# Thirty-two tile transposes taken off TensorE: VectorE turns 32 by 32 blocks, DMA through DRAM puts the blocks in place

## The chip, the cores and the metric

The kernel runs on one core of one Trainium2 chip. The metric is the device time of the launch in microseconds, median of the runs; lower is better. The profile is one execution of the program with the hardware profiler on.

## The reference, cut to what matters

Three blocks follow one another on four sequences of 576 tokens with 512 channels, all in 32-bit floats.

```python
# attention with a threshold: only scores within tau of the row's maximum count
attn_out = _attn_ref(q, k, v, tau)
...
# channel block
u = x + real(fft(fft(x, axis=1), axis=2))
un = (u - mean(u)) / sqrt(var(u) + 1e-06)          # over the 512 channels
x3 = u + relu(un @ w_ch1) @ w_ch2                  # 512 -> 2048 -> 512
# token block
theta = x3 @ w_theta
y = w_tok_r @ (x3 * cos(theta)) + w_tok_i @ (x3 * sin(theta))   # over the 576 tokens
u = x3 + y
out = u + relu(u @ w_ch)
```

## The kernel before, in words

**Arithmetic.** Matrix products are done in a rounded 32-bit form. Each operand is split into a high part (a rounding cast on ScalarE) and a low part (a subtraction on VectorE or GpSimd), and a product takes three passes: high by high, high by low, low by high.

**Stages.** Attention runs over 16 pairs of heads, with the Fourier transforms of the four sequences woven in (`attention_and_fft`). Its result u goes to DRAM as 18 tiles of 128 tokens by 512 channels (`u_d`, stores L876 and L921). `channel_mlp` reads them back in five chunks (`CHUNKS`, of 4, 4, 4, 3 and 3 tiles). `token_mix` reads the 18 tiles of its result x3 (`x3_d`) and works sequence by sequence, b = 0 to 3.

**A layer-norm tile** (`norm`, L1088 to L1144) is loaded into one of two buffers `un` (L1096), gets its statistics on VectorE (L1101, L1102), a root on GpSimd (L1106 to L1108) and its scaling on ScalarE or VectorE (L1113, L1115). Four TensorE transposes of 128 by 128 (L1120) put its channels on the partitions, in one PSUM bank; ScalarE casts the bank to the high part `uh` (L1127) and VectorE subtracts for the low part `ul` (L1131). `uh` and `ul` of a chunk lie in tiles b16 and b17, or b18 and b19, by turns.

**The channel products** (`unit`) go over 16 slices f of the hidden 2048 in each chunk. `first` is 12 matmuls (L1158) into a bank h. ScalarE makes `hh` of it (relu and cast, L1163), VectorE makes `hl` (L1167). `second` is three matmuls for each tile of the chunk (L1178 to L1180). On TensorE's queue, which runs in order, first(f+1) stands ahead of second(f). After slice 15, `leave` adds the reloaded u on VectorE (L1208) and stores the x3 tile (L1211).

**A token tile** (`token`, L1272 onward) is loaded from `x3_d` into `tok` (L1280), turned by four TensorE transposes (L1285), split into `xs` high and low (L1289 on ScalarE, L1292 on VectorE), and copied turned into `x3T` for the sequence (L1298, for the two tail tiles L1302). The theta product is 12 matmuls (L1310); then come five VectorE steps (L1314 to L1329), three ScalarE steps (L1332 to L1338), two products with the unturned tile (L1342) and the split into z (L1380, L1383). `mix` multiplies z by the token weights (L1434, 216 matmuls for each sequence), adds into `x3T` in place (L1452 to L1455) and splits the sum (L1468 to L1479). `final` is 12 matmuls at a time (L1498) whose result is added to `x3T` on VectorE (L1505 to L1510) and stored (L1513). `x3T` has two places, b18 and b16, so sequence 2 takes over the place of sequence 0, and 3 that of 1.

**Order.** Nothing is issued in source order. Each piece of work is an operation with the engines that may do it, a cost, a priority, what it comes after and which buffers it makes or uses (`Plan.op`, L130). `Plan.schedule` (L137) plays the program through with these costs and fixes for every engine, SyncE's DMA queue (SP) among them, one order; each queue then runs in that order and waits on semaphores. A tile load is entered as 800 ns of SP with a `delay` of 2500 ns until it has landed. `SHIFT` (from L1578 on) is a table of some 400 offsets that are added to priorities. `Plan.PORT` (L106) names the operations in which VectorE and GpSimd are not planned at the same time.

Of the kernel before, what the change touches and what calls it, by code (L numbers as in the profile page):

```python
# [9 lines left out]
F32 = mybir.dt.float32  # L10
# [88 lines left out]
class Plan:  # L99
# [888 lines left out]
def channel_mlp(pl, tc, ident, tb, pss, P2, wf, u_d, x3_d, w3, w3_d):  # L988

    nc = tc.nc  # L990
    for t, n in dict(raw2=2, rawe=1, ve=1, v0=1, v1=1, sh=1, un=2, hh=2, hl=2, hh2=2, hl2=2).items():
        pl.tag(t, n)
# [3 lines left out]
    wt, X, acc, R = {}, {}, {}, {}  # L996
# [88 lines left out]
    def stored(t):  # L1085
        return [("us", t)] if t < 16 else [("us", t, 0), ("us", t, 1)]

    def norm(ci, j, p0):  # L1088
# [47 lines left out]
        pl.op(("nl", k), "SP", 800, p0, load, stored(t), [u], delay=2500)  # L1136
        pl.op(("n0", k), "DVE", 830, p0 + 1, stats, [("nl", k)], (), [u])
        pl.op(("n1", k), "POOL", 1400, p0 + 1, root, [("n0", k)])
        pl.op(("n2", k), (("ACT", act(512, False)), ("DVE", 460)), 0, p0 + 2, scale, [("n1", k)], (), [u])
        pl.op(("n3", k), "PE", 428, p0 + 3, turn, [("n2", k)] + ([("first", (ci - 2, NF - 1))] if ci > 1 else []) +  # L1140
# [54 lines left out]
    def leave(ci):  # L1195
# [29 lines left out]
def token_mix(pl, tc, ident, tb, pss, P2, w3_d, x3_d, out):  # L1225
# [46 lines left out]
    def token(t, p0):  # L1272
# [3 lines left out]
        T, O = ("O", "T", "tok", t), ("O", "tok", t)  # L1276
# [5 lines left out]
        def turn(e):  # L1282
            loc["T"] = pl.bank([128, 4, 128], f"xT{t}")
            for c in range(4):
                e.transpose(loc["T"][:, c], loc["t"][:, 0, c * 128:c * 128 + 128], ident[:])  # L1285

        def hi(e):
            loc["x"] = new("v0", [128, 2, 4, 128], f"xs{t}", F32R)
            e.copy(loc["x"][:, 0], loc["T"][:])  # L1289

        def lo(e):
            e.tensor_sub(loc["x"][:, 1], loc["T"][:], f32(loc["x"][:, 0]))  # L1292

        def keep(e):
            if i < 4:
                if i == 0:
                    xT[b] = new(X_TAG[b % 2], [128, 4, 512], f"x3T{b}")
                e.copy(xT[b][:, :, i * 128:i * 128 + 128], loc["T"][:])  # L1298
            else:
                if t == 16:  # L1300
                    XT[0] = new("v1", [128, 4, 256], "xtail")
                e.copy(XT[0][:, :, 64 * b:64 * b + 128], loc["T"][:])  # L1302
# [114 lines left out]
    def mix(b, c, halves):  # L1417
# [31 lines left out]
        def add(e):  # L1449
# [3 lines left out]
            if 1 in halves:  # L1453
# [5 lines left out]
              [("mix", b, c, halves, 8), ("tk", 16 + b // 2)] + [("tk", 4 * b + i) for i in range(4)], (), [ps, xtile(b), XTT])  # L1459
# [78 lines left out]
class Late:  # L1538
# [186 lines left out]
    (('bound', 15, 8), -199.02), (('bound', 2, 8), -206.66), (('bound', 3, 0), -61.74), (('bound', 3, 3), -109.26),  # L1725
    (('bound', 6, 6), -61.18), (('bound', 9, 2), -85.32), (('bound', 9, 5), 220.4), (('bound', None, 3), 53.52),
# [241 lines left out]
```

## Time and profile before

| what | value |
|---|---|
| median of 3 runs | 976.63 us (973.43 to 978.11) |
| the profiled execution, its own time | 976.14 us |
| its span, first to last instruction | 974.4 us |
| TensorE matmuls busy | 952.7 us (98%) |
| VectorE, ScalarE, GpSimd busy | 604.1, 449.7, 298.6 us |
| mean granted clock | 0.998 |

A matmul's duration in the profile covers its whole way through the array, and the next one starts before it ends. So the sum of durations counts overlaps twice, while the chain of waits gives each instruction the time that it alone adds. A group's row has its line, engine, operation, output and inputs, shapes and count, then busy time and mean, then idle time before it and what ended that. The windows' rows have, for each stretch, each engine's busy time and count, the granted clock, the mean share of the 16 DMA engines and GB/s.

### The profile page before, as it was taken

The page shows a single profiled execution, that of the slowest core. Times are in us where ns is not written, and L with a number is a line of the kernel's source. Part 1 is how long each engine was busy: PE and PEld are TensorE (multiplying, and loading weights), DVE is VectorE, ACT ScalarE, POOL GpSimd, SP SyncE. Part 2 cuts the span into 40 slices and gives each one's busy share as a digit, 9 for nine tenths or more (in the row PEclk, how much of TensorE's full clock was granted, in tenths as well). Part 3 has the DMA queues.
Part 4 walks back from the last instruction along what each step waited for, and adds up shares of the span by engine and source line. Part 5 has one row for each costly group of instructions (what it writes and reads, how often), then busy time and mean ns, then how long its engine had stood idle before and what let it go on. Part 6 is the DMA issues. An engine that isn't in the chain of part 4 may idle for free.

```text
span 974.4 us, 15966 instructions
## 1 busy us (share of the span) xinstructions
PE 952.7 (98%) x5874; PEld 819.9 (84%) x5874; DVE 604.1 (62%) x1206; ACT 449.7 (46%) x851; POOL 298.6 (31%) x457
## 2 busy tenths in 40 slices
PE   8899999999899999999999999999999999999998
PEld 6676788777778788888888888899988999999998
DVE  6777888898898898665432451311255478676633
ACT  7677877777877545433221321111143245352410
POOL 3375755657563774543300110000001011000100
PEclk9999999999999999999999999999999999999999
DMA  6798548755681566435733440100336101111011
GB/s 186 200 224 209 141 111 222 203 149 145 181 209 61 169 202 225 136 121 198 251 126 106 149 166 17 55 1 1 141 128 223 63 23 47 46 41 53 11 50 50
DMA packets 52142, 122.74 MB, mean 126 GB/s; under 512 B 9440, under 2 KB 14240, under 8 KB 51680
## 3 DMA queue, kind: packets, MB, share of 16 engines
q1 hardware_dynamic: 51040, 118.08, 41.1%
q0 software_dynamic: 720, 2.76, 1.1%
q8 instruction: 47, 0.77, 0.3%
q10 hardware_dynamic: 304, 0.87, 0.3%
q14 instruction: 31, 0.25, 0.1%
HBM read 68.95 MB, written 23.66 MB: 95 GB/s over the span
## 4 chain that ended last, share of the span: by engine, by line
PE 81%; DMA 4%; DVE 3%; ACT 1%; issue 1%; POOL 1%; SPq 0%; DVEq 0%; ACTq 0%
PE h L1158 20%; PE y L1434 12%; PE acc L1180 7%; PE acc L1179 7%; PE acc L1178 7%; PE f L1498 5%; PE th L1310 5%; PE O L571 5%; PE T L501 3%; PE ps L469 2%; DMA u_d<-u 2%; PE ps L470 2%; PE ps L464 1%; DMA mu<-u_d 1%; PE Xo L775 1%; DVE P L494 1%
## 5 line engine op out<-in xcount | busy, mean ns | idle before, releaser
L1158 PE MATMUL h<-uh,w 128*128 128x512 f32 (+1 forms) x640 | 198.6, 371 | 0.0
L1167 DVE SCALAR_TENSOR_TENSOR hl<-h,hh 128x512 fp32r<-128x512 f32 (+1 forms) x80 | 50.8, 637 | 170.6 <-ACT hh L1163 166.0
L1163 ACT ACTIVATE hh<-h 128x512 fp32r<-128x512 f32 (+1 forms) x80 | 44.4, 555 | 240.6 <-PE h L1158 180.7
L1158 PEld LDWEIGHTS h<-uh,w 128*128 128x128 f32 x640 | 118.9, 188 | 16.7
L494 DVE SCALAR_TENSOR_TENSOR P<-ps,c,P 128x576 f32<-128x576 f32 x144 | 115.3, 814 | 14.7 <-ACT P L483 10.4
L478 DVE TENSOR_REDUCE c<-ps 128x1 f32<-128x576 f32 x144 | 106.2, 751 | 25.5 <-PE ps L470 16.4
L1158 PE MATMUL h<-ul,w 128*128 128x512 f32 (+1 forms) x320 | 118.1, 369 | 0.0
L483 ACT ACTIVATE P<-ps,c 128x576 f32<-128x576 f32 x144 | 106.3, 751 | 19.2 <-DVE c L478 15.7
L1178 PE MATMUL acc<-w,hh 128*128 128x512 f32 x288 | 113.7, 395 | 0.0
L1180 PE MATMUL acc<-w,hl 128*128 128x512 f32 x288 | 112.9, 392 | 0.0
L1179 PE MATMUL acc<-w,hh 128*128 128x512 f32 x288 | 112.6, 391 | 0.0
L1434 PE MATMUL y<-w,z 128*128 128x288 f32 x768 | 109.3, 296 | 0.0
L1434 PEld LDWEIGHTS y<-w,z 128*128 128x128 f32 x768 | 104.2, 188 | 0.7
L501 PE MATMUL T<-ident,P 128*128 128x128 f32 x576 | 84.2, 275 | 6.4 <-ACT pt L510 2.3
L510 ACT COPY pt<-T 128x512 f32<-128x512 f32 (+1 forms) x160 | 83.8, 555 | 10.7 <-PE T L501 9.8
L571 PE MATMUL O<-pt,vr 128*64 128x320 f32 (+1 forms) x640 | 85.8, 415 | 0.5 <-ACT R L624 0.5
L501 PEld LDWEIGHTS T<-ident,P 128*128 128x128 f32 x576 | 66.4, 140 | 14.1 <-ACT pt L510 6.5
L469 PE MATMUL ps<-H,L 128*128 128x288 f32 x240 | 75.4, 331 | 1.3 <-DVE P L494 0.5
L571 PEld LDWEIGHTS O<-pt,vr 128*64 128x64 f32 x640 | 43.5, 138 | 32.1 <-issue 4.3
L1342 POOL TENSOR_TENSOR tok<-tok 128x512 f32<-128x512 f32 x5 | 6.5, 1298 | 204.1 <-ACT tok L1338 175.7
L1158 PEld LDWEIGHTS h<-ul,w 128*128 128x128 f32 x320 | 60.1, 188 | 8.5
L470 PE MATMUL ps<-X,L 128*128 128x288 f32 x240 | 66.9, 295 | 0.0
(354 smaller groups left out, 1738.0 us busy)
## 6 DMA issues: line engine op xcount, KB each, us to landing
raw<-in_qk SPq DMA_DIRECT2D x14, 608.0 KB
vr<-in_vv SPq DMA_DIRECT2D x16, 384.0 KB
w<-w_d SPq DMA_DIRECT2D x6, 992.0 KB
H<-hs SPq DMA_DIRECT2D x30, 160.0 KB
X<-raw SPq DMA_DIRECT2D x30, 160.0 KB
X<-hs SPq DMA_DIRECT2D x30, 160.0 KB
H<-raw SPq DMA_DIRECT2D x30, 160.0 KB
mu<-u_d SPq DMA_DIRECT2D x18, 256.0 KB
```

The costliest lines, as they stand in the source:

```text
L469: e.matmul(ps[:, half, :HS], L[:, qo:qo + 128], H[:, ko:ko + HS], start=(j == 0), stop=False)
L470: e.matmul(ps[:, half, :HS], L[:, qo:qo + 128], X[:, ko:ko + HS], start=False, stop=(j == n - 1))
L478: e.tensor_reduce(loc["c4"][:, 0:1], loc["ps"][:, :, :HS], axis=AXES.XY, op=ALU.max, negate=True)
L483: e.activation(halves(), loc["ps"][:, :, :HS], AF.Exp, bias=loc["c4"][:, 0:1], scale=1.0)
L494: e.scalar_tensor_tensor(halves(), loc["ps"][:, :, :HS], loc["c4"][:, 1:2], halves(), op0=ALU.is_ge, op1=ALU.mult, accum_out=st["sums"][:, ...
L501: e.transpose(T[:, kt * 128:(kt + 1) * 128], P[:, kt * 128:(kt + 1) * 128], ident[:])
L571: e.matmul(O[64 * h:64 * h + 64, :n], w, x, start=(kt == 0), stop=(kt == 4))
L1158: e.matmul(loc["ps"][:, :n], a, x[:, c, :n], start=(k == 0), stop=(k == 11))
L1178: e.matmul(a, hh[:, q], wh, start=(f == 0), stop=False)
L1179: e.matmul(a, hh[:, q], wl, start=False, stop=False)
L1180: e.matmul(a, hl[:, q], wh, start=False, stop=(f == NF - 1))
L1434: e.matmul(loc["ps"][:, half, :HS], z[:, cs], w, start=(n == 0 and m == 0), stop=(n == 8 and m == 2))
```

## The change

14 of the 18 layer-norm tiles (chunks 1 to 4) and all 18 token tiles are no longer turned by TensorE. VectorE transposes each 32 by 32 block of a tile in its place (`flip`, into a single buffer `ut`). Four DMAs (`unfold`) write the blocks to a DRAM tile of 512 by 128, in runs of 32 floats, so that the tile lies there transposed. One DMA reads it back (`fetch`). For a layer-norm tile it lands in `ul`; ScalarE casts it to `uh` and VectorE or GpSimd subtracts in place. For a token tile the flip and the four DMAs are issued behind the addition of L1208 at the end of the chunk; the fetch lands in `x3T` directly, the split reads it there, and the copies of L1298 and L1302 go. The unturned load (L1280) stays, and is now awaited by the first VectorE step after theta. The subtraction for `xs` low may run on GpSimd. Some 300 lines of offsets in `SHIFT`, over all stages and attention's operations among them, are replaced by others.

```diff
+def unfold(e, d, src):
+    for i in range(4):
+        e.dma_start(d[:].rearrange("(b r) (i k)->i r b k", r=32, i=4)[i],
+                    src[32 * i:32 * i + 32].rearrange("r (b k)->r b k", k=32))
...
+        if ci:
+            def flip(e):
+                loc["b"] = new("ut", [128, 512], f"un{t}")
+                e.transpose(loc["b"][:], loc["u"][:])
+            def put(e):
+                unfold(e, un_d[t], loc["b"])
+            def fetch(e):
...
+                e.dma_start(f32(X[ci][1][:, :, q]), un_d[t][:].rearrange("(c p) k->p c k", c=4))
+            def hi2(e):
+                e.copy(X[ci][0][:, :, q], f32(X[ci][1][:, :, q]))
+            def lo2(e):
+                uh, ul = X[ci]
+                e.tensor_sub(ul[:, :, q], f32(ul[:, :, q]), f32(uh[:, :, q]))
+            ut = ("ut", ("n", t))
+            pl.op(("nf", k), "DVE", dve(512), p0 + 3, flip, [("n2", k), "attention done"], [ut], [u])
+            pl.op(("ns", k), "SP", 2480, p0 + 3, put, [("nf", k)], (), [ut], delay=2500)
+            pl.op(("nt", k), "SP", 800, p0 + 3, fetch, [("ns", k)] + ([("first", (ci - 2, NF - 1))] if ci > 1 else []) +
...
+            pl.op(("n4", k), "ACT", act(512, False), p0 + 3, hi2, [("nt", k)], (), cs)
+            pl.op(("n5", k), (("POOL", pool(512)), ("DVE", dve(512))), 0, p0 + 3, lo2, [("n4", k)], (), cs)
+            return
...
+            def flip(e, j=j, t=t):
+                B[t] = new("ut", [128, 512], f"xt{t}")
+                e.transpose(B[t][:], R[ci][:, j])
+            def put(e, t=t):
+                unfold(e, xt_d[t], B[t])
+            ut = ("ut", ("x", t))
+            pl.op(("xf", t), "DVE", dve(512), p0 + 0.2, flip, [("x3", t)], [ut], [raw])
+            pl.op(("xp", t), "SP", 2480, p0 + 0.3, put, [("xf", t)], (), [ut], delay=2500)
...
-        def turn(e):
-            loc["T"] = pl.bank([128, 4, 128], f"xT{t}")
-            for c in range(4):
-                e.transpose(loc["T"][:, c], loc["t"][:, 0, c * 128:c * 128 + 128], ident[:])
+        def fetch(e):
+            if i == 0:
+                xT[b] = new(X_TAG[b % 2], [128, 4, 512], f"x3T{b}")
...
+            e.dma_start(here(), xt_d[t][:].rearrange("(c p) k->p c k", c=4))
         def hi(e):
             loc["x"] = new("v0", [128, 2, 4, 128], f"xs{t}", F32R)
-            e.copy(loc["x"][:, 0], loc["T"][:])
+            e.copy(loc["x"][:, 0], here())
...
-        op("tt", "PE", 428, p0 + 2, turn, [("tl", t)], [T], [tk])
-        op("th", "ACT", act(512), p0 + 2.1, hi, [("tt", t)], [xp], [T])
-        op("to", "DVE", dve(512), p0 + 2.2, lo, [("th", t)], (), [T, xp])
-        op("tk", "ACT", act(512), p0 + 2.3, keep, [("tt", t)] + before, fresh, [T] + ([] if fresh else [kept]))
+        op("tx", "SP", 800, p0, fetch, [("xp", t)] + before, fresh, [] if fresh else [kept], delay=2500)
+        op("th", "ACT", act(512, False), p0 + 2.1, hi, [("tx", t)], [xp], [kept])
+        op("to", pool_or_dve(512), 0, p0 + 2.2, lo, [("th", t)], (), [kept, xp])
```

## Rows read from the trace of the kernel before

**Rows 1.** The page: span, and busy time of each engine.
```profile
span 974.4 us, 15966 instructions
PE 952.7 (98%) x5874; PEld 819.9 (84%) x5874; DVE 604.1 (62%) x1206; ACT 449.7 (46%) x851; POOL 298.6 (31%) x457
```

**Rows 2.** The windows: attention, channel products, changeover, token stage.
```profile
0.00:330.00 330.00, 312.72 (x2341) 250.47 (x2342) 271.57 (x643) 250.60 (x512) 193.24 (x371) 0.99 0.67 173
330.00:700.00 370.00, 369.03 (x1760) 312.75 (x1759) 172.29 (x235) 102.53 (x149) 88.45 (x74) 1.00 0.38 129
700.00:765.00 65.00, 65.00 (x328) 57.48 (x327) 31.93 (x53) 23.71 (x42) 5.16 (x4) 1.00 0.42 147
765.00:965.00 200.00, 200.00 (x1408) 193.47 (x1408) 126.08 (x270) 72.83 (x148) 11.70 (x9) 1.00 0.13 38
```

**Rows 3.** The chain of waits, pieces in order of time (start, us, what).
```profile
443.85 0.44 PE uT L1120 x4
...
891.45 0.44 PE xT L1285 x4
```

**Rows 4.** Groups of TensorE: the token tiles' transposes, as durations.
```profile
L1285 PE MATMUL xT<-ident,tok 128*128 128x128 f32 x72 | 10.8, 272 | 0.0
```

**Rows 5.** The timeline of TensorE around one set of transposes (start, us).
```profile
613.06 0.60 PE L1120 MATMUL uT<-ident,mu 128*128 128x128 f32 x4
613.42 0.48 PE L1178 MATMUL acc<-w,hh 128*128 128x512 f32 x1
```

**Rows 6.** Groups of VectorE, ScalarE and GpSimd with tiles of 128 by 512.
```profile
L1383 DVE TENSOR_TENSOR z<-tok,z 128x512 fp32r<-128x512 f32 x24 | 18.1, 762 | 0.9 <-ACT z L1380 0.2
L1329 DVE TENSOR_SCALAR tok<-tok 128x512 f32<-128x512 f32 x18 | 7.6, 425 | 0.4
L1383 POOL TENSOR_TENSOR z<-tok,z 128x512 fp32r<-128x512 f32 x8 | 10.4, 1303 | 64.5 <-ACT z L1380 56.8 <-issue 7.7
L1289 ACT CAST xs<-xT 128x512 fp32r<-128x512 f32 x18 | 10.5, 586 | 30.6 <-PE xT L1285 20.1 <-PE th L1310 10.4
```

**Rows 7.** Groups behind `first` in a chunk of four tiles.
```profile
L1163 ACT ACTIVATE hh<-h 128x512 fp32r<-128x512 f32 x48 | 28.7, 599 | 147.7 <-PE h L1158 112.5 <-PE acc L1179 35.2
L1167 DVE SCALAR_TENSOR_TENSOR hl<-h,hh 128x512 fp32r<-128x512 f32 x48 | 33.0, 690 | 92.4 <-ACT hh L1163 87.8 <-PE uT L1120 4.4
```

**Rows 8.** The chain's `first` of two moments, and DMA share of the stretches around them.
```profile
489.24 2.72 PE h L1158 x12
...
597.33 2.76 PE h L1158 x12
...
488.00:502.00 14.00, 14.00 (x64) 11.58 (x62) 5.59 (x8) 4.34 (x5) 1.86 (x1) 1.00 0.45 145
596.00:604.00 8.00, 8.00 (x36) 6.52 (x35) 1.38 (x2) 1.20 (x2) 0.00 (x0) 1.00 0.00 0
```

**Rows 9.** Timelines of SyncE and VectorE: a load, and what awaits it.
```profile
580.80 0.32 SPq L1096 DMA_DIRECT2D mu<-u_d  x1
...
583.82 0.69 DVE L1101 BATCH_NORM_STATS2 bs<-mu 128x6 f32<-128x512 f32 x1 [1.53 <-DMA mu<-u_d]
```

**Rows 10.** What SyncE's queue waited for (us in total, times, longest).
```profile
SPq L1211 <- DVE ru L1208: 103.6, 18, 66.0
```

**Rows 11.** The page: the packets of SyncE's queue over the whole span.
```profile
q1 hardware_dynamic: 51040, 118.08, 41.1%
```

**Rows 12.** The DMA view of 38.9 to 39.3 us: 256-byte packets, 0.4 us of 16 engines.
```profile
DMA packets 82, 0.02 MB, mean 49 GB/s; under 512 B 81, under 2 KB 81, under 8 KB 82
q1 hardware_dynamic: 82, 0.02, 28.2%
```

**Rows 13.** Timelines of TensorE and ScalarE: theta of tile 8; its copy into x3T.
```profile
818.69 2.92 PE L1310 MATMUL th<-w,xs 128*128 128x512 f32 x12
...
831.22 0.59 ACT L1298 COPY x3T<-xT 128x512 f32<-128x512 f32 x1 [3.07 <-DVE o L1509]
```

More of the change, by code (lines that the diff above doesn't have):

```diff
@@ L985, with channel_mlp @@
          ("y", 1, 0): 20, ("y", 1, 1): 21, ("u", 1, 0): 22, ("u", 1, 1): 23}
-def channel_mlp(pl, tc, ident, tb, pss, P2, wf, u_d, x3_d, w3, w3_d):
+def unfold(e, d, src):
+    for i in range(4):
+        e.dma_start(d[:].rearrange("(b r) (i k)->i r b k", r=32, i=4)[i],
+                    src[32 * i:32 * i + 32].rearrange("r (b k)->r b k", k=32))
+def channel_mlp(pl, tc, ident, tb, pss, P2, wf, u_d, x3_d, w3, w3_d, un_d, xt_d):
     nc = tc.nc
-    for t, n in dict(raw2=2, rawe=1, ve=1, v0=1, v1=1, sh=1, un=2, hh=2, hl=2, hh2=2, hl2=2).items():
+    for t, n in dict(raw2=2, rawe=1, ve=1, v0=1, v1=1, sh=1, un=2, hh=2, hl=2, hh2=2, hl2=2, ut=1).items():
         pl.tag(t, n)
@@ L1135, in norm @@
         cs = [(a, ("c", ci)), (b, ("c", ci))]
-        pl.op(("nl", k), "SP", 800, p0, load, stored(t), [u], delay=2500)
-        pl.op(("n0", k), "DVE", 830, p0 + 1, stats, [("nl", k)], (), [u])
+        nl = ("Nl" if ci else "nl", k)
+        pl.op(nl, "SP", 800, p0, load, stored(t), [u], delay=2500)
+        pl.op(("n0", k), "DVE", 830, p0 + 1, stats, [nl], (), [u])
         pl.op(("n1", k), "POOL", 1400, p0 + 1, root, [("n0", k)])
         pl.op(("n2", k), (("ACT", act(512, False)), ("DVE", 460)), 0, p0 + 2, scale, [("n1", k)], (), [u])
+        if ci:
[5 more added lines that the diff above has]
+            def fetch(e):
+                if j == 0:
+                    X[ci] = (new(a, [128, 4, 512], f"uh{ci}", F32R), new(b, [128, 4, 512], f"ul{ci}", F32R))
+                e.dma_start(f32(X[ci][1][:, :, q]), un_d[t][:].rearrange("(c p) k->p c k", c=4))
[8 more added lines that the diff above has]
+            pl.op(("nt", k), "SP", 800, p0 + 3, fetch, [("ns", k)] + ([("first", (ci - 2, NF - 1))] if ci > 1 else []) +
+                  (["fft done"] if ci % 2 and not j else []) + ([("nt", (ci, 0))] if j else []), [] if j else cs, cs if j else [],
+                  delay=2500)
+            pl.op(("n4", k), "ACT", act(512, False), p0 + 3, hi2, [("nt", k)], (), cs)
+            pl.op(("n5", k), (("POOL", pool(512)), ("DVE", dve(512))), 0, p0 + 3, lo2, [("n4", k)], (), cs)
+            return
         pl.op(("n3", k), "PE", 428, p0 + 3, turn, [("n2", k)] + ([("first", (ci - 2, NF - 1))] if ci > 1 else []) +
@@ L1222, in channel_mlp, with token_mix @@
         leave(ci)
-def token_mix(pl, tc, ident, tb, pss, P2, w3_d, x3_d, out):
+def token_mix(pl, tc, ident, tb, pss, P2, w3_d, x3_d, xt_d, out):
     pl.tag("ul3", 1)
@@ L1280, in load, with here @@
             e.dma_start(loc["t"][:, 0], x3_d[t])
-        def turn(e):
-            loc["T"] = pl.bank([128, 4, 128], f"xT{t}")
-            for c in range(4):
-                e.transpose(loc["T"][:, c], loc["t"][:, 0, c * 128:c * 128 + 128], ident[:])
+        def here():
+            return xT[b][:, :, i * 128:i * 128 + 128] if i < 4 else XT[0][:, :, 64 * b:64 * b + 128]
+        def fetch(e):
+            if i == 0:
+                xT[b] = new(X_TAG[b % 2], [128, 4, 512], f"x3T{b}")
+            if t == 16:
+                XT[0] = new("v1", [128, 4, 256], "xtail")
+            e.dma_start(here(), xt_d[t][:].rearrange("(c p) k->p c k", c=4))
         def hi(e):
             loc["x"] = new("v0", [128, 2, 4, 128], f"xs{t}", F32R)
-            e.copy(loc["x"][:, 0], loc["T"][:])
+            e.copy(loc["x"][:, 0], here())
         def lo(e):
[L1292 to L1302, printed above, removed]
+            e.tensor_sub(loc["x"][:, 1], here(), f32(loc["x"][:, 0]))
         def theta(e):
@@ L1458, in mix @@
         pl.op(("y", b, c, halves), "DVE", sum((dve(HS), dve(n2) + dve(64))[half] for half in halves), p1, add,
-              [("mix", b, c, halves, 8), ("tk", 16 + b // 2)] + [("tk", 4 * b + i) for i in range(4)], (), [ps, xtile(b), XTT])
+              [("mix", b, c, halves, 8), ("tx", 16 + b // 2)] + [("tx", 4 * b + i) for i in range(4)] +
+              [("to", 16 + b // 2)] + [("to", 4 * b + i) for i in range(4)], (), [ps, xtile(b), XTT])
         for half in halves:
@@ L1733 @@
-    (('exp', 2), -15.61), (('exp', 2, 6), 12.94), (('exp', None, 1), 5.82), (('exp', None, 3), -36.91),
[10 rows of a table removed]
-    (('fh', 2, 'o', 0), -133.99), (('first', 0, 3), -830.59), (('first', 1), 34.88), (('first', 1, 0), -33.34),
-    (('first', 3), -12.53), (('first', 3, 0), -29.48), (('first', 4, 7), 28.8), (('first', None, 13), 7.61),
[3 rows of a table removed]
-    (('guard',), 5.4), (('guard', 10), 80.15), (('guard', 14), 38.44), (('guard', 3), -95.63), (('hh', 0), -25.85),
[13 rows of a table removed]
-    (('mix',), 4.26), (('mix', 0), -58.41), (('mix', 1, 0, (0, 1), 1), 36.65), (('mix', 1, 0, (0, 1), 7), 29.14),
@@ L1764 @@
-    (('mix', 1, 1, (0, 1)), 18.65), (('mix', 1, 1, (0, 1), 0), -48.46), (('mix', 1, 1, (0, 1), 5), -4.22),
-    (('mix', 1, 2, (0, 1), 7), 85.31), (('mix', 1, 3, (0, 1)), 27.13), (('mix', 1, 3, (0, 1), 8), 37.56),
-    (('mix', 1, None, (0, 1)), -0.94), (('mix', 2, 0), 16.76), (('mix', 2, 0, (0, 1), 2), -51.66),
-    (('mix', 2, 3, (0, 1), 0), -36.01), (('mix', 3), -43), (('mix', 3, 0, (0,)), 38.09),
-    (('mix', 3, 0, (1,), 1), 28.54), (('mix', 3, 3, None, 5), 4.87), (('mix', 3, None, (0,)), -21.8),
@@ L1769 @@
-    (('mix', None, 1, (0, 1), 8), 69.66), (('mix', None, None, (0,)), 2.75), (('mix', None, None, None, 4), -27.99),
-    (('mix', None, None, None, 6), -16.91), (('mix', None, None, None, 8), -21.88), (('n0',), 66.84),
[4 rows of a table removed]
-    (('second',), 4.08), (('second', 1, 15), -20.89), (('second', 2, 14), -36.09), (('second', 2, 15), -49),
-    (('ta', 5), -38.19), (('to', 12), -98.66), (('tt', 12), -5.48), (('tt', 2), 14.63), (('tt', 4), -32.47),
-    (('turn', 0), -23.27), (('turn', 0, 0), -71.58), (('turn', 0, 2), -101.88), (('turn', 0, 4), -84.45),
@@ L1788 @@
-    (('turn', 7, 0), 54.24), (('turn', 7, 3), -4.57), (('turn', 7, 4), 17.15), (('turn', 7, 'r'), -26.59),
-    (('turn', 8, 'r', 0), 53.41), (('turn', 9, 3), 23.18), (('turn', 9, 4), 19.38), (('turn', 9, 5), 873.6),
-    (('turn', 9, 'r'), -15.99), (('turn', None, 0), -10.1), (('turn', None, 4), 1.48), (('turn', None, 6), 8.19),
-    (('turn', None, 7), 3.88), (('turn', None, 8), -2.5), (('turn', None, None, 0), -6.1),
-    (('turn', None, None, 2), 9.79), (('turn', None, 'r', 0), -1.92), (('turn', None, 'r', 1), -15.35),
@@ new lines @@
+    (('evac', 2, 2), 163.27), (('evac', 3, 8), -187.58), (('evac', None, 3), 39.3), (('exp',), -39.47),
+    (('exp', 0), -196.98), (('exp', 0, 0), -8.7), (('exp', 0, 3), 56.52), (('exp', 0, 6), 230.59),
+    (('exp', 0, 7), 2.61), (('exp', 1), -112.02), (('exp', 1, 5), 26.07), (('exp', 13, 3), 4.13),
+    (('exp', 2, 6), 81.45), (('exp', None, 3), -32.63), (('exp', None, 6), -30.61), (('f', 0, 0, 2), -35.3),
[23 rows of a table added]
+    (('lq',), 99.58), (('lq', 13), -172.62), (('mask',), -263.71), (('mix',), 29.4), (('mix', 0), -37.87),
@@ new lines @@
+    (('mix', 1, 1, (0, 1), 0), -48.46), (('mix', 1, None, (0, 1)), 35.27), (('mix', 2), 8.04), (('mix', 2, 0), 34.55),
+    (('mix', 2, 0, (0, 1), 6), -45.47), (('mix', 2, 1, (0, 1), 0), -48.61), (('mix', 2, 3), 10.11),
+    (('mix', 2, 3, (0, 1), 0), -35.51), (('mix', 3), -37.24), (('mix', 3, 0, (1,), 1), 28.54),
+    (('mix', 3, 2, (0,), 2), 61.86), (('mix', 3, 2, (1,), 0), 6.83), (('mix', 3, 3), -27.24),
+    (('mix', 3, 3, (0,), 4), 123.76), (('mix', 3, None, (0,)), -18.45), (('mix', None, 0, (0,)), 16.78),
@@ new lines @@
+    (('mix', None, 1), 8.23), (('mix', None, 2), -3.57), (('mix', None, 3, (0, 1)), -18.42),
+    (('mix', None, None, (0, 1), 3), 21.65), (('mix', None, None, None, 4), -31.4),
+    (('mix', None, None, None, 6), -16.91), (('mix', None, None, None, 8), -21.88), (('mu',), -57.35),
[5 rows of a table added]
+    (('pv', None, 1), -1.05), (('raw', 14), 887.04), (('second',), 100.06), (('second', 0, 3), -9.15),
+    (('ta',), -11.33), (('ta', 15), 38.24), (('ta', 6), -37.65), (('th', 2), -1.14), (('th', 5), 5.51),
+    (('to', 15), -59.55), (('turn',), -0.21), (('turn', 0), -18), (('turn', 0, 0), -63.36), (('turn', 0, 2), -75.35),
@@ new lines @@
+    (('turn', 0, 4), -84.45), (('turn', 0, 8), -26.78), (('turn', 1), 4.39), (('turn', 1, 1), -27.98),
+    (('turn', 1, 3), -25.11), (('turn', 1, 'r'), -37.67), (('turn', 1, 'r', 0), 73.17), (('turn', 10), -0.52),
+    (('turn', 10, 0), 22.35), (('turn', 10, 8), -16.57), (('turn', 10, 'r', 0), 51.5), (('turn', 11, 1), -6.85),
+    (('turn', 11, 4), 29.86), (('turn', 11, 7), -11.17), (('turn', 11, 'r'), -37.32), (('turn', 12, 3), 4.28),
+    (('turn', 12, 'r', 2), -14.67), (('turn', 13), 5.71), (('turn', 13, 2), -21.03), (('turn', 13, 4), 5),
@@ new lines @@
+    (('turn', 13, 'r'), -32.17), (('turn', 14), 11.94), (('turn', 14, 0), 29.77), (('turn', 14, 4), 48.66),
+    (('turn', 14, 7), 21.5), (('turn', 14, 'r', 0), 39.36), (('turn', 15), 9.24), (('turn', 15, 1), 23.1),
+    (('turn', 15, 4), 51.96), (('turn', 15, 7), -16.46), (('turn', 2), -5.42), (('turn', 2, 2), -5.61),
+    (('turn', 3), -2.84), (('turn', 3, 6), 21.81), (('turn', 3, 7), -28.91), (('turn', 3, 8), 8.67),
+    (('turn', 4, 0), 39.97), (('turn', 4, 5), -11.37), (('turn', 4, 6), 6.08), (('turn', 4, 'r', 2), -20.66),
@@ new lines @@
+    (('turn', 5, 1), -6.64), (('turn', 5, 4), 27.32), (('turn', 5, 6), 97.24), (('turn', 5, 'r', 1), 138.54),
+    (('turn', 6), 5.02), (('turn', 6, 1), -9.5), (('turn', 6, 4), 13.33), (('turn', 6, 5), 72.2),
+    (('turn', 6, 'r', 2), 30.33), (('turn', 7, 0), 52.88), (('turn', 7, 6), -48.38), (('turn', 8, 1), -6.83),
+    (('turn', 8, 5), -6.33), (('turn', 8, 'r', 0), 53.41), (('turn', 8, 'r', 2), -18.89), (('turn', 9, 3), 36.09),
+    (('turn', 9, 5), 873.6), (('turn', 9, 'r', 2), 5.09), (('turn', None, 0), -10.96), (('turn', None, 3), 1.46),
@@ L1795 @@
+    (('turn', None, 6), 1.04), (('turn', None, None, 0), -9.37), (('turn', None, None, 2), 5.29),
[6 rows of a table added]
 )
@@ L1825, in body @@
         x3_d = [dram.tile([128, 512], F32, name=f"x3_d{i}") for i in range(NT)]
+        un_d = [dram.tile([512, 128], F32, name=f"un_d{i}") for i in range(NT)]
+        xt_d = [dram.tile([512, 128], F32, name=f"xt_d{i}") for i in range(NT)]
         w3_d = [dram.tile([128, 2, W3W[i]], F32, name=f"w3_d{i}") for i in range(NW3)]
@@ L1858, in body @@
             pl.op("fft done", None, 0, 901, turn_over(left, "c"), transform + ["attention done"])
-            channel_mlp(pl, tc, ident, tb, pss, late, wf, u_d, x3_d, w3, w3_d)
-            token_mix(pl, tc, ident, tb, pss, late, w3_d, x3_d, out)
+            channel_mlp(pl, tc, ident, tb, pss, late, wf, u_d, x3_d, w3, w3_d, un_d, xt_d)
+            token_mix(pl, tc, ident, tb, pss, late, w3_d, x3_d, xt_d, out)
             pl.emit()
```

32 lines of the change are left out of this document (9 added, 23 removed), and 119 rows, old and new, of the table SHIFT.

## Prediction

> **What bounds the kernel now.** I read the page first: of a span of 974.4 us TensorE's matmuls fill 952.7 us, VectorE's work 604.1 us, ScalarE's 449.7 us and GpSimd's 298.6 us [rows 1]. A share over the whole span mixes stages, so the windows come next, and there the reader should see two kernels. From 330 to 965 us TensorE is busy 369.0, 65.0 and 200.0 us in stretches of 370, 65 and 200 us: without a gap, at the full granted clock of 1.00, which is 2.4 GHz. VectorE is busy 330 us of these 635 us (172.3 + 31.9 + 126.1). Before 330 us TensorE stands idle for 17.3 us (330 less 312.7) and VectorE is busy for 271.6 us: there it is a race of several engines [rows 2]. All that the change edits lies in the first kind of stage, except the order. In such a stage an instruction taken off TensorE shortens the time by what it adds to TensorE's chain, as long as nothing else comes late.
>
> **What is removed.** 14 layer-norm tiles and 18 token tiles lose four transposes each: 32 sets. The chain of waits gives one set 0.44 us, in the channel stage as in the token stage [rows 3]. So 32 x 0.44 = 14.1 us. This is the main term, and it has two other readings. By durations a transpose is 0.15 us of busy time (10.8 us for 72), so 128 of them would be 19.2 us; but durations overlap [rows 4]. By starts, the matmul behind a set begins 0.36 us after the set's first transpose, so 32 sets would be 11.5 us; but that matmul is itself late with its weights: it takes 0.48 us [rows 5]. I take 14.1, with 11.5 and 19.2 as ends.
>
> **What is added to VectorE, ScalarE and GpSimd.** 32 flips of 128 by 512. No row shows a transposing VectorE operation; operations on tiles of this size take from 0.43 us (one operand) to 0.76 us [rows 6]. I take 0.69 us, the price of the plain pass of `hl` [rows 7]: 22 us beside some 305 us in which VectorE is idle after 330 us. The subtraction of `xs` or `ul` may go to GpSimd, where a like one takes 1.30 us instead of about 0.7 us [rows 6], on an engine that is busy 5 of 65 us and 12 of 200 us there [rows 2]. ScalarE loses 18 copies of some 0.59 us, the price of the like cast [rows 6]. None of this is on the path, because TensorE's own queue covers it. If that cover goes, a flip costs what `hl` is late by: TensorE has one `first` of 2.72 us [rows 8] between the end of a `first` and the `second` that needs its `hl`, and ScalarE and VectorE use 0.60 and 0.69 us of it [rows 7]. So 1.4 us of lateness on VectorE is free, and more is paid in full.
>
> **What is added to the queues.** Each of the 32 tiles gets four DMAs to DRAM and one back: 160 DMAs, at 0.32 us of issue each [rows 9] 51 us of SP's time. SP has it: it stood 103.6 us in waits for the x3 additions alone [rows 10]. Behind a fetch that waits on SP for its blocks stand the next u loads, weight loads and x3 stores; they are due many microseconds later, so a wait of a few microseconds there is costed at nothing. A tile now moves 2,048 packets of 128 bytes and 512 of 512 bytes, in all 81,920 against 51,040 packets on this queue before [rows 11]. Their price is the unknown. The nearest row has packets of 256 bytes between tiles on the chip: 82 packets take 28.2% of 0.4 us of 16 engines, 22 ns each [rows 12]. The far end is the mean packet of the queue, 2.3 KB: 41.1% of 16 x 974.4 us for 51,040, 126 ns [rows 11]. At 22 ns all of it is 113 us of each engine's time, at 126 ns 645 us; after 330 us the engines are busy for 0.38 x 370 + 0.42 x 65 + 0.13 x 200 = 194 of 635 us [rows 2], so the near end fits beside the rest and the far one does not. I take 22 ns, because the packet's length is nearest to that row's. The extra traffic as such does not slow TensorE: `first` takes 2.72 us where the DMA share is 0.45 and 2.76 us where it is 0.00 [rows 8].
>
> **The new round trip.** A load is used 3.0 us after its issue [rows 9]; its eight packets for each engine at 126 ns are 1.0 us of that, so 2.0 us are fixed. The four DMAs are then 2.0 + 128 x 0.022 = 4.8 us; the plan allows 2.48 + 2.5 = 4.98 us. The fetch (32 packets for each engine) is under the load's 3.0 us. With flip and splits a tile is ready 10 us after its scaling, where the bank was ready at once. A chunk of four tiles is 32 runs of 12 matmuls, 87 us at 2.72 us each [rows 8], and a chunk's tiles can be turned while the one before it is computed, so this is hidden; costed at nothing.
>
> **A rule against the change.** The row's 256-byte packets stay on the chip, and these go to DRAM. The Trainium skill (DMA: Bandwidth & Descriptors, Specifications) says that a transfer needs 512 bytes for line rate and that below this the DMA engine does a read-modify-write. No row here shows such writes to DRAM. By the row the sum stays at 14.1 us saved; by the rule it would be the first rival below.
>
> **The order.** The offsets change for attention's operations too, and no row can price that. The most that order can win before 330 us is TensorE's idle time there, 17.3 us [rows 2]. I take 0, with half of it, 8.6 us, as an end on either side.
>
> **Sum.** The profiled execution took 976.14 us (span 974.4 and 1.7 us around it): 976.14 - 14.1 = 962.0 us. It lies 0.5 us below the median, so against the median of 976.63 I forecast 962.5 us.
>
> **Rivals.** *VectorE blocked by the single buffer (slower).* `ut` is one buffer: the next flip waits until the four DMAs of the last have landed, and on VectorE's queue `hl` stands behind it. Flips come in a row where a chunk ends and where a chunk's tiles are normed: of 32, all but the first at five chunk ends, 27. A put may exceed its planned 4.98 us by the 1.4 us of slack, so 6.4 us is free: 34 ns for each packet. If each write needs a read as well, a packet is twice 22, 44 ns, and the put 2.0 + 5.6 = 7.6 us; each flip stalls TensorE for 1.2 us, 27 x 1.2 = 33 us, and the time is 976.6 - 14.1 + 33 = 995 us. It decides from where 27 stalls outweigh 14.1 us: 0.5 us each, a packet of 39 ns. This is what the page's rule above would do. For it: the single buffer, and writes shorter than any to DRAM so far. Against: the 22 ns row. 10%.
>
> *The token tile's place comes late (no change).* Before, theta of tile 8 started at 818.7 us from the PSUM bank, though its place in `x3T` came free only for the copy at 831.2 us, behind sequence 0's last addition [rows 13]. Now the fetch itself needs the place. If TensorE then waits for fetch, cast and subtraction (3.0 + 0.6 + 1.3 = 4.9 us) at the changes to sequence 2 and 3, 9.8 us come back: 972.3 us. For it: TensorE's order is fixed, and these two places do bind. Against: `mix` of the sequence between, 216 matmuls, is there to be done meanwhile. 12%.
>
> *The order wins too (faster).* Half of the idle time before 330 us goes: 962.5 - 8.6 = 953.9 us. For it: 17.3 us of idle time are there. Against: attention's own work is untouched. 12%.
>
> **How the numbers follow.** My forecast, with the order's end on the slow side in it, has 66%. A measurement of this kernel can tell about 0.5%, 4.9 us, from no change. Faster than 971.7 us: the forecast except 2%, the order's win, and 3% of the second rival, 0.79. Within 4.9 us: the rest of these two, 0.11. Slower than 981.5 us: the first rival, 0.10. The range reaches from 952, just past the order's win, to 973, past the second rival and the slow ends of the main term (965.1) and of the order (971.1); it leaves out the first rival and some of the order's tail.
>
> **What would show it.** Right: after 330 us TensorE still busy without a gap, no L1285 left, L1120 with 16 transposes, matmul pitch unchanged, the span shorter by some 14 us and nearly all of it after 430 us. The flip's mean should lie between 0.43 and 0.76 us, and VectorE's wait for the block DMAs should be near nothing. Wrong: idle time of TensorE ended by `hl` with VectorE itself waiting for a DMA of `ut` (first rival); idle time before L1310 at the changes of sequence (second); or a gain or loss that lies before 330 us (order).

## The result, and the profile after

The changed kernel took 961.04 us (958.75 to 962.43, 4 runs) beside 975.89 us of the kernel before: a ratio of 0.9846, with a 95% interval from 0.9812 to 0.988. It is faster by 14.9 us; 962.5 was forecast. Run again later beside the experiments it took 958.42 us, 0.9829 [0.9806, 0.9851]. The profiled execution took 962.40 us.

The page, in the lines that answer to [rows 1] and [rows 11]:

```profile
span 960.5 us, 15977 instructions
PE 937.9 (98%) x5746; PEld 807.1 (84%) x5746; DVE 626.9 (65%) x1225; ACT 441.7 (46%) x835; POOL 301.9 (31%) x468
q1 hardware_dynamic: 135520, 134.87, 50.9%
```

TensorE has 128 matmuls fewer and is 14.8 us less busy; its idle time hardly changed (974.4 - 952.7 = 21.7 us before, 22.6 us now). VectorE has 22.8 us more work, ScalarE 8.0 us less. SyncE's queue carries 84,480 packets more.

The windows after, as in [rows 2]:

```profile
0.00:330.00 330.00, 313.92 (x2357) 253.10 (x2358) 274.97 (x643) 250.53 (x515) 192.17 (x380) 1.00 0.67 174
330.00:700.00 370.00, 369.34 (x1737) 314.06 (x1737) 195.27 (x263) 105.28 (x153) 78.53 (x67) 1.00 0.57 161
700.00:765.00 65.00, 64.11 (x327) 56.16 (x326) 40.14 (x66) 25.23 (x43) 2.78 (x2) 1.00 0.58 180
765.00:951.00 186.00, 185.45 (x1295) 178.87 (x1294) 114.50 (x246) 60.64 (x126) 28.38 (x21) 1.00 0.19 55
```

From 330 us on TensorE is busy without a gap worth naming, as before. The new work shows beside it: in the second row VectorE has 195.3 us instead of 172.3, and the DMA engines' share rose from 0.38 to 0.57.

The groups of the flips:

```profile
L1251 DVE STREAM_TRANSPOSE xt<-ru 128x512 f32<-128x512 f32 x18 | 12.7, 705 | 10.4 <-DMA xt_d<-xt 10.3
L1150 DVE STREAM_TRANSPOSE un<-mu 128x512 f32<-128x512 f32 x14 | 9.8, 703 | 1.0 <-DMA un_d<-un 0.7 <-ACT mu L1119 0.3
```

What TensorE waited for from 330 us on, all of it (us, times, longest):

```profile
PE th L1351 <- ACT xs L1340: 0.9, 1, 0.9
PE f L1539 <- DVE tok L1362: 0.5, 1, 0.5
PE Xo L775 <- DVE u L836: 0.4, 1, 0.4
PE Xo L775 <- DVE glo L716: 0.2, 1, 0.2
```

The single buffer does hold VectorE up, 10.3 + 0.7 us in all, and none of that reaches TensorE: neither `hl` nor `hh` is in its list.

One round trip, in the timelines of VectorE and of SyncE's queue (start, us):

```profile
435.68 0.70 DVE L1251 STREAM_TRANSPOSE xt<-ru 128x512 f32<-128x512 f32 x1
436.60 0.69 DVE L1203 SCALAR_TENSOR_TENSOR hl<-h,hh 128x512 fp32r<-128x512 f32 x1 [0.21 <-ACT hh L1199]
439.99 0.71 DVE L1251 STREAM_TRANSPOSE xt<-ru 128x512 f32<-128x512 f32 x1 [2.71 <-DMA xt_d<-xt]
```

```profile
436.41 1.95 SPq L990 DMA_DIRECT2D xt_d<-xt  x4
```

The put's first issue is at 436.41 us and the next flip may start at 439.99: 3.6 us, of which SyncE needs 1.95 us to issue the four DMAs. The first two of them, taken one by one:

```profile
436.41 0.32 SPq L990 DMA_DIRECT2D xt_d<-xt  x1
436.77 0.49 SPq L990 DMA_DIRECT2D xt_d<-xt  x1
```

The first is issued as fast as a plain load before the change (0.32 us, [rows 9]). Over all 32 puts the medians of the first to the fourth are 0.32, 0.49, 0.51 and 0.51 us, and a plain load or store issued straight behind a block DMA has a median of 0.50 us too (13 of them). So the longer issue belongs to what stands behind a block DMA, whatever its own shape. `hl` came between the two flips and was in time. In the stretch of 1 us from 612.5 us, where block packets are nearly alone, the DMA view has

```profile
DMA packets 484, 0.06 MB, mean 64 GB/s; under 512 B 482, under 2 KB 482, under 8 KB 484
...
q1 hardware_dynamic: 484, 0.06, 41.4%
```

so 0.414 x 16 x 1.0 us / 484 = 13.7 ns of an engine for a packet.

### The profile page after: what moved, and what is told of

The parts are those of the page before. It is cut to its first block, busy times and chain, and to the rows that moved or that the text cites. A ratio compares the mean times of both kernels' runs of the same rounds, so it can differ in the third digit from the quotient of the medians.

```text
span 960.5 us, 15977 instructions
## 1 busy us (share of the span) xinstructions
PE 937.9 (98%) x5746; PEld 807.1 (84%) x5746; DVE 626.9 (65%) x1225; ACT 441.7 (46%) x835; POOL 301.9 (31%) x468
## 4 chain that ended last, share of the span: by engine, by line
PE 80%; DVE 5%; ACT 3%; DMA 2%; issue 1%; SPq 0%; DVEq 0%; POOL 0%
PE h L1194 20%; PE y L1474 12%; PE acc L1216 7%; PE acc L1214 7%; PE acc L1215 7%; PE f L1539 5%; PE th L1351 5%; PE O L571 5%; PE T L501 3%; PE ps L469 2%; PE ps L470 2%; DVE P L494 1%; DVE c L478 1%; ACT P L483 1%; PE ps L464 1%
## 5 line engine op out<-in xcount | busy, mean ns | idle before, releaser
L1474 PE MATMUL y<-w,z 128*128 128x288 f32 x768 | 106.9, 294 | 0.0
L571 PE MATMUL O<-pt,vr 128*64 128x256 f32 (+1 forms) x640 | 84.7, 411 | 0.5 <-ACT R L624 0.5
L1216 PEld LDWEIGHTS acc<-w,hl 128*128 128x128 f32 x288 | 54.1, 188 | 11.8
```

The source lines that it names most:

```text
L571: e.matmul(O[64 * h:64 * h + 64, :n], w, x, start=(kt == 0), stop=(kt == 4))
L1216: e.matmul(a, hl[:, q], wh, start=False, stop=(f == NF - 1))
L1474: e.matmul(loc["ps"][:, half, :HS], z[:, cs], w, start=(n == 0 and m == 0), stop=(n == 8 and m == 2))
```

## The experiments

Two theories stood against each other after the result. Mine: the gain is the 32 sets of transposes, each by what it adds to TensorE's chain, and the new order is worth nothing. The rival: the new offsets made much of it, the sets lie in slack. The runs were made in three groups, each beside its own runs of the kernel before, with medians of 975.6 to 976.2 us; across groups they are compared by their ratios to that kernel.

**The offsets apart from the rest.** One kernel is the changed one with the table of offsets of before; the other is the kernel before with the new table.

```diff
-SHIFT = (...)        # offsets of the changed kernel
+SHIFT = (...)        # offsets of the kernel before
```

> The changed kernel with the old table of priority offsets. If the gain is TensorE's freed chain alone (32 sets of 0.44 us) and the order is worth nothing: about 962 us, 13 to 15 us below the kernel before. If the new order carries a good part of the gain: 966 to 975 us, with the difference to the changed kernel in TensorE's idle time before 330 us.

> The kernel before, transposes on TensorE, with the new table of priority offsets. If the order is worth nothing by itself: 976 us, within 3 us of the kernel before. If the order carries the gain: 962 to 970 us.

Measured: 980.86 us, 1.0041 [1.0016, 1.0066], and 990.17 us, 1.0136 [1.0104, 1.0168]. Both parts alone are slower than the kernel before, and together they are faster. Both expectations missed, mine and the rival's: the offsets carry no gain that can be added to or taken from the change. The planner plays the whole program through, so an operation more or less moves everything behind it: with the old offsets the changed kernel runs in the order of the kernel before for the first 224 us, on TensorE, VectorE, ScalarE and GpSimd, and then drifts away from it. A table is worth something only with the program that it was fitted to: the changed program loses 20 us with the old one.

In the run with old offsets TensorE's waits are many and short (us, times, longest; the longest five of those before 330 us):

```profile
PE T L541 <- DVE P L494: 2.5, 2, 1.4
PE T L501 <- ACT pt L510: 2.3, 5, 0.7
PE ps L464 <- DVE P L494: 2.2, 1, 2.2
PE T L541 <- ACT pt L510: 2.0, 3, 0.8
PE T L541 <- DVE u L836: 1.5, 1, 1.5
```

No single wait explains the 20 us. TensorE is idle for 979.6 - 945.0 = 34.6 us of that span, 12 us more than in the changed kernel, and busy for 7 us more with the same matmuls. Of those 7 us some 4.3 are the clock's, by an estimate from the windows (busy time by the missing share): the granted clock was 0.66 from 90 to 95 us, 0.76 from 345 to 352 and 0.66 from 930 to 935. The rest stays open.

**Dead transposes put back.** The changed kernel keeps its order on every other engine, and TensorE alone gets transposes that nobody reads: 14 sets ahead of `first`, 18 ahead of theta.

```diff
+            if ci and f < len(CHUNKS[ci]):
+                for c in range(4):          # range(16), with c % 4 below, in the other run
+                    e.transpose(loc["ps"][:, c * 128:c * 128 + 128], ident[:], ident[:])
...
             loc["ps"] = pl.bank([128, 512], f"th{t}")
+            for c in range(4):              # the same there
+                e.transpose(loc["ps"][:, c * 128:c * 128 + 128], ident[:], ident[:])
```

> The changed kernel with 32 sets of four transposes of the identity put back on TensorE, 14 ahead of a product of the channel stage and 18 ahead of a theta product, into the bank that the product then overwrites; nobody waits for them. If a set is worth the chain's 0.44 us and TensorE's queue is the bound throughout: 961.0 + 14.1 = 975.1 us, 13.5 to 15 us above the changed kernel. By the distance of starts (0.36 us): +11.5 us. By the durations (0.60 us): +19.2 us. If TensorE had slack: under +8 us.

> The kernel after the change, with sixteen dead transposes of the identity where the run of dead turns had four, at the same 32 places; every other engine keeps its order. Left out: nothing, the transposes write banks that the next matmuls clear. The change alone took 961.0 us, the run with four at each place 973.7. Theory: each transpose on TensorE's full queue costs its slot (0.09 us by the starts in the run with four, 0.11 by the chain's 0.44 us a set), plus some 0.07 us a place for the matmul behind, paid once. So 384 more transposes cost 34 to 42 us: 1008 to 1016 us. Rival by durations (0.15 us each): 58 us, 1031 us. Rival that the 12.7 us of the first run were mostly a disturbance at each place (the weights of the matmul behind, a late split) and not the transposes: under 20 us more, below 994 us.

> The kernel after the change once more, unchanged, so that it stands beside the other runs on the same chip. 959 to 963 us, 0.985 of the kernel before; with it the runs with dead turns can be compared without going by two ratios.

Measured: 973.72 us, 0.9971 [0.995, 0.9993], with four; 1015.63 us, 1.0418 [1.0394, 1.0441], with sixteen; 958.42 us for the change again, just under the 959 to 963 expected. Against the change again, 32 sets cost 0.0142 x 975.6 = 13.9 us, 0.43 us each, and 128 sets cost 57.2 us, 0.45 us each. From the one to the other 384 transposes add 0.0447 x 975.6 = 43.6 us, 0.114 us each. By the intervals of the ratios each of these differences is good to some 3 us, so the four alone would not tell 0.44 us for a set from 0.36; the sixteen do. The theory by slots (1008 to 1016 us) holds; durations (1031 us) and a cost for each place (below 994 us) fall.

The chain of waits shows the same price, first with four, then with sixteen (start, us, what):

```profile
442.41 0.44 PE h L1192 x4
442.85 2.80 PE h L1197 x12
```

```profile
428.87 1.75 PE h L1192 x16
...
952.63 1.75 PE th L1351 x16
```

0.44 us for four, 1.75 us for sixteen: 0.11 us for a transpose at the first place and at the last, while the groups give each 0.272 us as its own duration.

**The old order kept by hand.** The changed kernel's operations get as priority their place in the plan of the kernel before, the new ones behind those that they follow, and an operation that two engines may do is held to one. The table `STARTS` has both.

```diff
+        table = json.loads(zlib.decompress(base64.b85decode(STARTS)))
+        for o in self.ops:
+            at = table.get(repr(o["name"]))
...
+            o["prio"] = at[0]
+            if at[1] is not None:
+                o["alts"] = tuple(a for a in o["alts"] if a[0] == at[1]) or o["alts"]
```

> The kernel after the change, with the operations of every queue put in the order of the kernel before by hand (each operation's place there is its priority), the new ones behind what they follow; so neither of the two orders that belong to a set of offsets is used. Theory (the gain is the 32 sets, the order costs only where it belongs to another program): 976 less 12 to 14, 962 to 966 us. Rival (the gain needs the new offsets): 972 us or more, as with the old offsets, 980.9 us.

Measured: 971.99 us, 0.9962 [0.9945, 0.998]. My 962 to 966 missed, and it came out at the edge of the rival's 972 or more. The order of before does better than its offsets do (980.86), yet of the 14 us that the sets are worth only 3.7 are left (0.0038 x 975.6): it gives back 10. Where, shows when each execution is cut at the start of chunk 0's `first`, behind which all that the change edits lies (starts from TensorE's timelines, the rest is the span less the start; each row is one execution):

| run | first starts, us | from there to the end, us |
|---|---|---|
| before | 327.72 | 646.7 |
| after | 325.53 | 635.0 |
| after, again | 322.33 | 633.5 |
| 32 dead sets | 323.74 | 648.6 |
| old order by hand | 330.29 | 640.8 |
| old offsets | 332.05 | 647.5 |
| new offsets, old kernel | 332.10 | 656.4 |

Put back in place, the sets bring the second part from 635.0 and 633.5 to 648.6, the 13.6 to 15.1 us again. The order of before gains 5.9 us there and starts 2.6 us later, behind a stage that the change doesn't edit. That the order costs these 2.6 us is not shown: in this execution the granted clock was 0.66 from 15 to 30 us, against 0.89 before, and over eight profiled executions that share the changed kernel's order a start lies anywhere from 322.1 to 328.2 us. So the middle column alone settles nothing finer.

**Puts sent two and four times.** The block DMAs of a tile go to unread DRAM tiles first, once or three times, and then to the real one. `ut` is held longer, which is the first rival's mechanism.

```diff
-def unfold(e, d, src):
+def unfold(e, d, src, more=True):
+    if more:
+        for _ in range(1):                  # 3 in the other run
+            unfold(e, JUNK.pop(), src, False)
```

> The changed kernel with each put sent four times, three of them to DRAM tiles that nobody reads; the plan is unaware of it. A put now takes 16 issues of 0.49 us and lands 9 to 10 us after its first issue, 4 to 5 us over the planned 4.98 us; SP's queue is held 6 us longer 32 times. Theory (the single buffer stands behind VectorE's queue, 1.4 us are free): a flip that follows another closely holds hl up by up to 3.4 us; with 13 to 27 such flips 40 to 90 us more, 1000 to 1050 us, with TensorE idle and hl as what ended it. Rival (the round trip is hidden with room to spare, since flips lie 5 us and more apart): 961 to 970 us.

> The kernel after the change, in which the four block DMAs of each tile are sent twice, the first time to a DRAM tile that nobody reads. The flip's buffer is held about twice as long: 3.6 us by the trace of the change become some 5.5 to 7 us, and SP issues 128 more DMAs of about 0.49 us, 63 us. With four sendings the time was 1112 us and TensorE waited 76 us for hh and hl. Theory (free up to 6.4 us, every microsecond above it is paid at up to 27 places): 961 to 980 us, TensorE's idle time ended by hl under 15 us. Rival (lateness is paid from the first microsecond, since SP's queue is late too, one step in a straight line to the run with four): a third of its 151 us, some 1011 us.

Measured: 1112.36 us, 1.1386 [1.135, 1.1423], with four sendings; 971.33 us, 0.9972 [0.995, 0.9994], with two, 12.9 us over the change. The change has a cliff, and it is near. What TensorE and ScalarE waited for with four sendings:

```profile
PE acc L1220 <- ACT hh L1205: 39.4, 8, 6.8
PE acc L1222 <- DVE hl L1209: 36.6, 13, 7.9
...
ACT uh L1167 <- DMA ul<-un_d: 74.1, 10, 19.0
```

and with two, from 330 us on, with VectorE's wait below:

```profile
PE acc L1220 <- ACT hh L1205: 4.7, 3, 1.8
PE h L1200 <- DVE w L1069: 1.6, 2, 0.8
PE acc L1222 <- DVE hl L1209: 1.6, 2, 1.0
...
DVE xt L1257 <- DMA xt_d<-xt: 44.1, 13, 6.0
...
ACT uh L1167 <- DMA ul<-un_d: 37.6, 10, 5.5
```

With two sendings the time lies in the theory's range, and the straight line's 1011 us falls. VectorE stands 44.1 us at the flips of L1257, and TensorE waits for `hl` for 1.6 us, in two waits of which neither leads back to a flip: that lateness is free. `hh` costs TensorE 4.7 us, in three waits. ScalarE stands 37.6 us at the cast of `uh`, for the fetch (14.4 us in the changed kernel, 6 times), but none of the three waits for `hh` comes of that. Each time `hh` stands on ScalarE's queue directly behind the rescaling of a piece of the token stage's weights (L1034), which waits for its own plain load (`raw`). For the first of the three, in the timelines of SyncE, ScalarE and TensorE:

```profile
502.58 0.50 SPq L1028 DMA_DIRECT2D raw('x', 4)_6283<-in_w  x1
...
507.74 1.09 ACT L1034 ACTIVATE v('x', 4)_6422<-raw('x', 4)_6283 128x992 f32<-128x992 f32 x1 [5.03 <-DMA raw('x', 4)_6283<-in_w]
508.73 0.59 ACT L1205 ACTIVATE hh<-h 128x512 fp32r<-128x512 f32 x1
...
509.37 0.50 PE L1220 MATMUL acc<-w,hh 128*128 128x512 f32 x1 [1.77 <-ACT hh L1205]
```

The doubled put holds SyncE's queue from 494.0 to 502.5 us, and the second half of this load is issued behind it. In the changed kernel the same step waited 1.3 us for its load, and `hh` was in time. So a second way had to be told from the buffer: lateness of what stands behind the puts on SyncE's queue, the fetch among it.

With four sendings the mechanism of the expectation is there: 40.6 us of TensorE's waits for `hl`, followed back along the queues, lead to a flip that waits for its buffer. Its size was too small, and the other way is there too: of the 39.4 us for `hh`, 17.9 lead to a fetch, 16.0 to loads of weights and 5.4 to a load of u. And the clock fell: the mean over the span is 0.949. Of the 149.2 us by which the span is longer than the changed kernel's (1109.7 - 960.5), TensorE's idle time has 103.5 us and its busy time, with the same matmuls, 45.7. The windows of that run around one stall:

```profile
485.00:490.00 5.00, 4.87 (x22) 3.67 (x20) 0.00 (x0) 0.60 (x1) 0.00 (x0) 1.00 0.81 119
490.00:495.00 5.00, 0.00 (x0) 0.00 (x0) 0.92 (x2) 0.00 (x0) 0.00 (x0) 0.89 0.53 77
495.00:500.00 5.00, 4.58 (x11) 3.61 (x12) 0.36 (x1) 0.00 (x0) 0.00 (x0) 0.50 0.71 105
```

TensorE did nothing from 490 to 495 us, and in the next stretch the granted clock is 0.50, which is 1.2 GHz: 11 matmuls in 5 us, where 22 went through at 1.00, 2.4 GHz.

**The buffer freed in time.** The unread DMAs stand behind the real ones and copy a finished tile of u between DRAM tiles, so that the flip's buffer shouldn't wait for its own tile's copies, while the fetch still does.

```diff
+    if more:
+        for _ in range(3):                  # 1 in the other run
+            unfold(e, JUNK.pop(), JUNK[0], False)
...
+        JUNK.insert(0, u_d[0])
```

> The kernel after the change; behind the four block DMAs of each tile, three times as many of the same size and form copy a finished tile of u between DRAM tiles, and nobody reads the result. SP's queue and the DMA engines carry as many block DMAs as with four sendings (1112 us), but the flip's buffer is free again as soon as its own four have landed; the fetch stands behind all sixteen. Theory (TensorE waits because VectorE stands at the next flip with hl behind it): most of the 151 us are gone, VectorE's wait for block DMAs is near the 11 us of the changed kernel, 965 to 1000 us. Rival (TensorE waits because the fetch is late and ScalarE stands at the cast of uh with hh behind it; there it waited 74 us in the run with four): 1050 us or more, with TensorE's idle time ended by hh.

> The same with one such set of four behind each put, to stand beside the run with two sendings (971.3 us, 12.9 us over the change alone; ScalarE waited 37.6 us there at the cast of uh for the fetch, VectorE 56 us at the flips). Theory (the buffer): 958 to 963 us, nothing lost. Rival (the late fetch): 967 to 972 us.

Measured: 1126.57 us, 1.1541 [1.1485, 1.1597], and 976.66 us, 0.9995 [0.997, 1.002]. With three copies the rival's range holds; with one the time lies above both ranges. With three copies TensorE waits for

```profile
PE acc L1220 <- ACT hh L1205: 68.8, 12, 8.7
PE acc L1222 <- DVE hl L1209: 14.3, 7, 3.9
...
ACT uh L1167 <- DMA ul<-un_d: 79.2, 9, 23.7
```

In the lines of L1220 and L1222 `hl` went from 36.6 to 14.3 us and `hh` from 39.4 to 68.8 us. The buffer was not freed as fully as meant: a flip still waits, because its predecessor's put stands on the queue behind the copies of the tile before. But VectorE's waits at the flips of L1257 fell by half, first with four sendings, then with three copies:

```profile
DVE xt L1257 <- DMA xt_d<-xt: 119.8, 13, 11.1
...
DVE xt L1257 <- DMA xt_d<-xt: 64.5, 10, 11.6
```

So they did from two sendings (44.1) to the single copy:

```profile
DVE xt L1257 <- DMA xt_d<-xt: 22.8, 9, 5.7
```

The time did not fall with them in either pair: 1.1541 after 1.1386, and 0.9995 after 0.9972, where the two intervals overlap. So the buffer alone doesn't set the loss. The rival's mechanism, the fetch, is there in part only: of the 68.8 us for `hh`, followed back along ScalarE's queue, 30.0 us lead to a fetch (5 waits), 31.6 to loads of weights (6) and 7.3 to a load of u (1).

What the change is sensitive to is SyncE's whole queue: the way from put to fetch, and every plain load that stands behind it. How much of the lateness is issue time and how much the transfers was not separated, and the copies read DRAM where the puts read the chip's own memory, so the two pairs are not alike to the microsecond.

## Why the prediction was right

**The main term was right to its size.** 0.44 us for a set, 14.1 us for 32, was taken from the chain; the dead sets cost 0.43 and 0.45 us, give or take some 3 us on each sum. The ends taken from starts (0.36, 11.5 us) and from durations (19.2 us) were both wrong readings. Of the gain that the two timings give, 14.9 and 17.2 us, the sets carry about 14.

**The order was not worth 0.** The run with 32 dead sets has TensorE's old work, the new order and the new work on the other engines. It is at 0.9971 [0.995, 0.9993], so order and new work together gain 2.8 us (0.7 to 4.9), inside the ends of 8.6 us. That is the remainder of the gain, and perhaps the third rival in small. The prediction's sign, nearly all of the gain after 430 us, held in part: chunk 1's `first` starts at 432.10 us before, and at 427.35 and 424.16 us in the two executions after, so 4.8 of 13.9 and 7.9 of 18.6 us were there by then. But the step took the order as a term of a sum, and that it isn't: with the wrong table the same change costs 4 us instead of gaining 15. The 0 for the order came out near enough by luck: no row priced it, and it holds only because each of the two kernels has a table that fits it. What no row of before could tell is that the change without new offsets would have been slower.

**The cover held.** The flip took 0.70 us (0.69 was taken), and no `hl` came late on TensorE. `first` still takes 2.72 us [rows 8], and so it does where the DMA engines are busy throughout, in the stretch from 488 to 502 us (the chain, and the window):

```profile
490.89 2.72 PE h L1194 x12
```

```profile
488.00:502.00 14.00, 14.00 (x63) 11.62 (x62) 8.20 (x8) 4.76 (x7) 4.01 (x3) 1.00 1.00 303
```

**The queues were mis-sized, without consequence.** The 160 DMAs were taken at 0.32 us of issue each, 51 us. Added up from the trace, the 128 block DMAs hold SyncE for 68.9 us and the 32 fetches for 14.2 us, 83 us in all: three of a put's four stand straight behind another, and single ones were held up to 2.3 us. A block packet took 13.7 ns instead of 22, so the put read above was 3.6 us instead of 4.8. The two errors pull opposite ways. Not every put ends inside the planned 4.98 us: the one at 484.33 us, where the DMA engines begin to be busy throughout, took 5.19 us to issue alone, and nothing on TensorE came late by it.

**The first rival didn't happen, and its point was misplaced.** A packet needed 39 ns and took 13.7. The Trainium skill (DMA: Bandwidth & Descriptors, Specifications) has a read-modify-write below 512 bytes; the 13.7 ns beside the 22 ns of [rows 12] show no time for one at these 128-byte writes. The rival's condition, a put over 6.4 us, was drawn for `hl` behind the flip. With two sendings VectorE waited 44 us at the flips of L1257, up to 6.0 us at one, and TensorE 1.6 us for `hl`: a late flip was not paid in full. What came late first was `hh`, behind loads of weights that stood on SyncE's queue behind the puts. These are the loads that the prediction had due many microseconds later and costed at nothing. That holds for the change as it stands, where 14.4 us of ScalarE's waits for the fetch are hidden as well, and not for twice the DMAs.

**The second rival didn't happen.** Theta of tile 8 does stand behind its fetch and cast, in the timelines of SyncE, ScalarE and TensorE:

```profile
821.21 0.38 SPq L1336 DMA_DIRECT2D x3T<-xt_d  x1
...
826.11 0.62 ACT L1340 CAST xs<-x3T 128x512 fp32r<-128x512 f32 x1 [4.68 <-DMA x3T<-xt_d]
...
820.56 6.50 PE L1474 MATMUL y<-w,z 128*128 128x288 f32 x48
826.90 3.17 PE L1351 MATMUL th<-w,xs 128*128 128x512 f32 x12
```

It moved from 818.7 [rows 13] to 826.9 us, and `mix` of the sequence between runs up to it; all waits for `xs` are 0.9 us instead of the rival's 9.8.

## What to carry to other kernels

Where one engine is busy without a gap, take the price of what leaves it from the chain of waits: 0.44 us for four transposes was right, their starts (0.36) and their durations (0.60) were not. An order that was fitted to a program belongs to it: price an edit together with its own order, and don't read an edit under the old order, or an order under the old edit, as its part of the gain. Work moved to an idle engine over a round trip through DRAM is free only as long as every in-order queue that waits for it is in time, and that takes in the plain loads behind it on the DMA queue: here ScalarE, standing for a load of weights, was late before VectorE at its flip. Sending the transfer twice is a quick measure of how far that is, and following a wait back to the DMA that ended it tells which load it was.

## What the runs showed that was not expected

128-byte packets to DRAM took 13.7 ns of an engine each, less than the 22 ns of 256-byte packets on the chip. A DMA of 64 KB in 128-byte runs is issued in 0.32 us when it stands first, like a plain tile load of 256 KB, but what is issued straight behind it takes some 0.50 us, a plain load too. And the loss from a busier SyncE queue is far from a straight line: one more set of block DMAs for each tile costs 13 us, three more cost 152 us (0.1557 x 976). Some two thirds of that are TensorE's idle time (103.5 us), and most of the rest goes with the lower granted clock behind its stalls.
